# A first weight load split in two and moved from ScalarE's DMA queue to SP's, in a two-layer Mish kernel

## The chip, the cores and the metric

The kernel runs on one core of a Trainium2 chip. The metric is the device time of one execution in microseconds. Before the change it was 105.13 us, the median of three runs (104.34 to 105.44). A core has TensorE (PE), VectorE (DVE), ScalarE (ACT), GpSimd (POOL) and SyncE (SP); each runs its own instructions in order, and they meet at semaphores. SP and ScalarE issue the DMAs here.

## The reference

```python
# x (1, 2048, 512), w1 (512, 1792), b1 (1792,), w2 (1792, 512), all bfloat16
h = jnp.einsum("bsd,df->bsf", x, w1) + b1
sp = jnp.log1p(jnp.exp(-jnp.abs(h))) + jnp.where(h > 0, h, jnp.zeros_like(h))
act = h * jnp.tanh(sp)                       # mish(h)
return jnp.einsum("bsf,fd->bsd", act, w2)
```

## The kernel before

The 2048 tokens are worked in four blocks of 512. In each block the first layer computes, for each of 14 f tiles (128 of the 1792 columns of w1), a 128x512 product over four k tiles (128 of the 512 input features each): `mm1_step`, L194, with w1 as the weights and the transposed x (`xT`) as the moving operand. ScalarE adds b1 and applies Mish (L200) into `a_sb`. The second layer (L252) multiplies `a_sb` with w2 into 128x512 output tiles, which ScalarE (L235) or, at the very end, VectorE (L238) copies out and SP stores (L242). The last ten tokens (eight in the later f tiles) are left out of the first layer's matmuls; VectorE computes them as dot products (`dots`, L213) from a transposed w1 (`w1T`) and broadcast rows of x (`xv`).

TensorE's order around the change: ten warm-up matmuls on constants (L157); eight transposes of the first 256 tokens (L169, `transpose_x`), which need the plain load `x_nat` and an identity from GpSimd; after each group of them VectorE copies the result into `xT` (L173), first k 0, then k 1, then k 2 and 3 together. Then the first layer of block 0 is done for these 256 tokens alone, first for f tiles 0-3 and then for 4-7 (`GROUPS`), and within a group k by k: four matmuls of k 0, four of k 1, and so on, 32 in all, each 256 columns wide. Then come tokens 256-511 for f tiles 0-7 (`xT` loaded by a DMA transpose), then f tiles 8-13 over all 512 tokens.

All loads go through `load` (L92): a DMA start with its own semaphore, which reaches 16 when all has landed. `load_w1` records for each pair (k, f) which semaphore a matmul must wait for. SP issues its loads one after the other from L128 on, ahead of everything else that it does, without waiting for any of them. ScalarE first waits for a memset of `b1_pad` by VectorE (L124), then issues w1's load for k 0-1 of f tiles 0-3, then b1 (L134), then loads its activation table (L151). b1 is turned on VectorE (L263 to L268) before the first Mish needs it.

Of the kernel before, what the change touches and what calls it, by code (L numbers as in the profile page):

```python
# [5 lines left out]
P = 128  # L6
# [28 lines left out]
def bass_standalone__dense_activation_mish__prompt_kernel(  # L35
# [14 lines left out]
    KT, FT = D // P, F // P  # L50
# [7 lines left out]
    with ExitStack() as es:  # L58
        def sb(name, shape, t):
            return es.enter_context(nc.sbuf_tensor(name, shape, t))  # L60
# [5 lines left out]
        b1_nat = sb("b1_nat", [FT, P], BF)  # L66
# [14 lines left out]
        def sem(name):  # L81
            return es.enter_context(nc.semaphore(name))

        sp = Stream(nc.sync, None)
        pe = Stream(nc.tensor, sem("c_pe"))
        dve = Stream(nc.vector, sem("c_dve"))
        act = Stream(nc.scalar, sem("c_act"))
        pool = Stream(nc.gpsimd, sem("c_pool"))

        def load(q, dst, src, name, transpose=False):  # L90
            s = sem(name)
            (q.eng.dma_start_transpose if transpose else q.eng.dma_start)(dst, src).then_inc(s, 16)  # L92
            return (s, 16)
# [3 lines left out]
        def load_w1(q, ks, a, b):  # L97
            t = load(q, w1_sb[:, ks, a * P:b * P], w1v[:, ks, a * P:b * P], "s_w1_%d_%d" % (ks.start, a))
            for f in range(a, b):
                for k in range(ks.start, ks.stop):  # L100
                    t_w1[k, f] = t

        def load_w2(a, b):
            t = load(sp, w2_sb[:, a:b, :], w2v[:, a:b, :], "s_w2_%d" % a)
            for f in range(a, b):
                t_w2[f] = t

        def load_xT(lo, hi):
            t = load(sp, xT[:, :, lo:hi], x2[lo:hi, :], "s_xT%d" % lo, True)
            for j in range(lo // P, hi // P):  # L110
                t_xT[j] = t
# [9 lines left out]
                t_xv[v] = t  # L121

        t_bz = dve.mark(nc.vector.memset(b1_pad[:, :], 0.0))  # L123
        act.wait(t_bz)  # L124

        x01 = x2[0:2 * P, :].rearrange("(p j) d -> p j d", j=2)
        out01 = out2[0:2 * P, :].rearrange("(p j) d -> p j d", j=2)
# [1 line left out]
        for a, b in GROUPS:  # L129
            if a == F0:  # L130
                load_xT(2 * P, 4 * P)
            for ks in (slice(0, 2), slice(2, KT)):
                load_w1(act if (a, ks.start) == (0, 0) else sp, ks, a, b)
        t_b1 = load(act, b1_nat[:, :], b1.rearrange("(j p) -> j p", p=P), "s_b1")  # L134
        load_w2(0, 5)
        load_w2(5, FT)
        load_xv(0, 4)
# [184 lines left out]
```

## Time and profile before

| | |
|---|---|
| median of three runs | 105.13 us (104.34 to 105.44) |
| the profiled execution | 104.65 us, its span 103.4 us |
| TensorE busy | 100.3 us, 97% of the span |
| VectorE, ScalarE busy | 76.9 us, 48.0 us |
| DMA | 11.11 MB moved, 107 GB/s in the mean; 331 to 379 GB/s in most slices of the first seventh |
| chain that ended last | 94% on TensorE, 3% on ScalarE |

Times in a row are microseconds from the span's start unless marked ns. L194 is line 194 of the kernel before. A tile's name in a row leaves numbers out: `w_sb` stands for w1 and w2, `b_nat` for b1. PEld is TensorE's weight load, which runs beside its matmuls. SPq and ACTq rows are the issuing of a DMA on SyncE and ScalarE. A matmul's row shows it longer than the distance to the next one, because they are pipelined: 0.31 us for a step of 0.107. A few matmul records are missing from the trace.

### The profile page before, as it was taken

Reading aid. Unit: us, or ns where it says so; the run is one execution under the profiler, and the core shown is the slowest. Engines: PE = TensorE matmul, PEld = TensorE weight load, DVE = VectorE, ACT = ScalarE, POOL = GpSimd, SP = SyncE. Lnnn points to the kernel's source line nnn. Section 1 sums busy time; section 2 is a strip of 40 time slices with the busy share of each in tenths; the row PEclk is TensorE's granted clock in tenths of the full one; section 3 lists DMA queues with packets and bytes.
Section 4 is the critical chain, followed back from the end, with each engine's and each line's share of the span. In section 5 each row is a group of like instructions: output and inputs, shape, how many; then the busy total and the mean of one; then the engine's idle time right before and its main releaser. Section 6 shows DMA issues by size and latency. Waiting matters only on the chain.

```text
span 103.4 us, 1446 instructions
## 1 busy us (share of the span) xinstructions
PE 100.3 (97%) x518; PEld 50.8 (49%) x526; DVE 76.9 (74%) x254; ACT 48.0 (46%) x75; POOL 0.7 (1%) x6
## 2 busy tenths in 40 slices
PE   6999999999999999999999999999999999999992
PEld 2798744444444444444444444444444444444492
DVE  0340000799999999999999999999999999980011
ACT  1305997201257777222227777522107888720220
POOL 2000000000000000000000000000000000000000
PEclk9999999999999999999999999999999999999999
DMA  2999999999999600011011000001111000001112
GB/s 80 331 294 362 349 379 137 375 262 190 216 245 230 213 6 0 0 51 45 6 51 51 3 0 0 10 0 51 51 51 51 0 0 0 0 6 51 51 51 51
DMA packets 21107, 11.11 MB, mean 107 GB/s; under 512 B 15340, under 2 KB 20716, under 8 KB 21100
## 3 DMA queue, kind: packets, MB, share of 16 engines
q1 hardware_dynamic: 20656, 10.73, 39.0%
q10 hardware_dynamic: 444, 0.29, 1.0%
q8 instruction: 4, 0.07, 0.2%
q14 instruction: 3, 0.02, 0.1%
HBM read 5.25 MB, written 2.10 MB: 71 GB/s over the span
## 4 chain that ended last, share of the span: by engine, by line
PE 94%; ACT 3%; issue 0%; ACTq 0%
PE ps L252 47%; PE ps L194 44%; ACT a_sb L200 3%; PE ps L157 3%; PE ps L169 1%; ACT o_sb L235 0%; ACTq L27 0%
## 5 line engine op out<-in xcount | busy, mean ns | idle before, releaser
L213 DVE SCALAR_TENSOR_TENSOR prod<-w1T,xv 128x512 f32<-128x512 bf16 x120 | 73.6, 684 | 12.2 <-DMA w1T<-in_w_dram 12.2
L194 PE MATMUL ps<-xT,w_sb 128*128 128x512 bf16 (+3 forms) x253 | 49.0, 353 | 0.2
L252 PE MATMUL ps<-w_sb,a_sb 128*128 128x512 bf16 (+3 forms) x247 | 48.6, 355 | 0.3
L200 ACT ACTIVATE a_sb<-ps,b_sb 128x512 bf16<-128x512 f32 (+2 forms) x56 | 37.3, 691 | 13.3 <-PE ps L194 13.3
L194 PEld LDWEIGHTS ps<-xT,w_sb 128*128 128x128 bf16 x256 | 25.1, 99 | 23.2 <-DMA w_sb<-in_w_dram 0.2
L252 PEld LDWEIGHTS ps<-w_sb,a_sb 128*128 128x128 bf16 x252 | 23.6, 98 | 25.2
L235 ACT ACTIVATE o_sb<-ps 128x512 bf16<-128x512 f32 (+1 forms) x16 | 9.2, 575 | 38.2 <-PE ps L252 38.2
L213 DVE DVE_READ_ACCUMULATOR prod<-w1T,xv 128x1 f32 x120 | 9.6, 80 | 0.0
L238 DVE CAST o_sb<-ps 128x256 bf16<-128x256 f32 (+1 forms) x2 | 0.7, 374 | 7.7 <-PE ps L252 7.7
L157 PE MATMUL ps<-const-bfloat16-1.0 128*128 128x512 bf16 (+1 forms) x10 | 2.8, 466 | 0.8 <-PEq L307 0.8
L173 DVE COPY xT<-ps 128x256 bf16<-128x256 bf16 (+1 forms) x3 | 0.9, 336 | 3.1 <-PE ps L169 2.9
L151 ACT ACT_TABLE_LOAD x1 | 1.3, 1283 | 2.2 <-issue 2.2
L157 PEld LDWEIGHTS ps<-const-bfloat16-1.0 128*128 128x128 bf16 x10 | 1.2, 139 | 2.2 <-issue 2.2
L169 PE MATMUL ps<-ident,x_nat 128*128 128x128 bf16 x8 | 1.1, 311 | 0.0
L266 DVE STREAM_TRANSPOSE b_t<-b_pad 32x32 bf16<-32x32 bf16 x4 | 0.8, 202 | 0.1
L169 PEld LDWEIGHTS ps<-ident,x_nat 128*128 128x128 bf16 x8 | 0.9, 147 | 0.0
L123 DVE MEMSET b_pad<- 32x64 uint32 x1 | 0.1, 112 | 0.9 <-PEq L307 0.9
L221 DVE TENSOR_TENSOR hb<-hv,b_sb 128x40 f32<-128x40 f32 (+1 forms) x2 | 0.4, 218 | 0.1
L263 DVE COPY b_pad<-b_nat 14x128 bf16<-14x128 bf16 x1 | 0.2, 182 | 0.3 <-DMA b_nat<-in_b_dram 0.3
L225 ACT ACTIVATE a_sb<-hb 128x40 bf16<-128x40 f32 (+1 forms) x2 | 0.4, 244 | 0.0
L149 POOL TENSOR_SCALAR_AFFINE_SELECT ident<-ones 128x128 bf16<-128x128 bf16 x1 | 0.3, 292 | 0.1
L147 POOL MEMSET ones<- 128x128 bf16 x1 | 0.2, 204 | 0.3 <-POOLq L307 0.3
(5 smaller groups left out, 0.6 us busy)
## 6 DMA issues: line engine op xcount, KB each, us to landing
out_dram<-o_sb SPq DMA_DIRECT2D x15, 128.0 KB, 1.7
w_sb<-in_w_dram SPq DMA_DIRECT2D x1, 1152.0 KB, 10.8
w_sb<-in_w_dram SPq DMA_DIRECT2D x3, 256.0 KB, 4.1
w_sb<-in_w_dram SPq DMA_DIRECT2D x2, 384.0 KB, 4.9
xv<-in_x_dram SPq DMA_DIRECT2D x1, 768.0 KB, 7.6
w_sb<-in_w_dram SPq DMA_DIRECT2D x1, 640.0 KB, 6.6
xv<-in_x_dram SPq DMA_DIRECT2D x1, 512.0 KB, 11.1
x_nat<-in_x_dram SPq DMA_DIRECT2D x1, 256.0 KB, 2.5
```

What stands on the lines that cost most here:

```text
L151: act.eng.preload_act_table(ACT.Mish)
L157: nc.tensor.matmul(ps[:, 7, 0:n], c_w, c_m[:, 0:n], start=True, stop=True)
L169: mm = nc.tensor.transpose(psb[:, (2 * i + j) * P:(2 * i + j + 1) * P], x_nat[:, j, k * P:(k + 1) * P], ident[:, :])
L173: t = dve.mark(nc.vector.tensor_copy(xT[:, ks[0]:ks[0] + n, 0:2 * P], psb[:, 0:2 * n * P].rearrange("p (k t) -> p k t", k=n)))
L194: return nc.tensor.matmul(ps[:, bank, lo:hi], w1_sb[:, k, f * P:(f + 1) * P], xT[:, k, starts[s] + lo:starts[s] + hi], start=first, stop=( ...
L200: t = act.mark(act.eng.activation(a_sb[:, f, starts[s]:starts[s] + width(s, f)], ps[:, bank, 0:width(s, f)], ACT.Mish, bias=b1_sb[:, f:f + ...
L213: t_dot[b] = dve.mark(nc.vector.scalar_tensor_tensor(prod[:, b, :], w1T[:, f, :], 1.0, xv[:, v, :], ALU.mult, ALU.mult, accum_out=hv[:, f, ...
L221: t = dve.mark(nc.vector.tensor_tensor(hb[:, a:b, v:NV], hv[:, a:b, v:NV], b1_sb[:, a:b].unsqueeze(2).to_broadcast([P, b - a, NV - v]), AL ...
L235: t = act.mark(act.eng.activation(o_sb[:, i, lo:hi], ps[:, bank, 0:hi - lo], ACT.Copy))
L238: t = dve.mark(nc.vector.tensor_copy(o_sb[:, i, lo:hi], ps[:, bank, 0:hi - lo]))
L252: mm = nc.tensor.matmul(ps[:, bank, 0:hi - lo], a_sb[:, f, i * P:(i + 1) * P], w2_sb[:, f, lo:hi], start=(f == 0), stop=(f == FT - 1))
L266: t_b1t = dve.mark(nc.vector.transpose(b1_t[c * 32:(c + 1) * 32, :], b1_pad[:, c * 32:(c + 1) * 32]))
```

## The change

The load of w1 for k 0 and 1 of f tiles 0-3 (256 KB) leaves ScalarE. It becomes two loads on SP, k 0 and k 1 apart (128 KB each), directly behind the load of x and ahead of all other loads of w1. ScalarE issues only b1, and without waiting for the memset. A matmul on k 0 now waits for the load of k 0 alone.

```diff
         t_bz = dve.mark(nc.vector.memset(b1_pad[:, :], 0.0))
-        act.wait(t_bz)
+        t_b1 = load(act, b1_nat[:, :], b1.rearrange("(j p) -> j p", p=P), "s_b1")
 ...
         for a, b in GROUPS:
             if a == F0:
                 load_xT(2 * P, 4 * P)
-            for ks in (slice(0, 2), slice(2, KT)):
-                load_w1(act if (a, ks.start) == (0, 0) else sp, ks, a, b)
-        t_b1 = load(act, b1_nat[:, :], b1.rearrange("(j p) -> j p", p=P), "s_b1")
+            for ks in (slice(0, 1), slice(1, 2), slice(2, KT)) if a == 0 else (slice(0, 2), slice(2, KT)):
+                load_w1(sp, ks, a, b)
         load_w2(0, 5)
```

What SP issues from the start of the program, before the change. `128x2x512` is two k tiles of 512 columns, `DMA_TRANSPOSE xT` the tokens 256-511, `x3` three such loads in a row.

```order
L92 DMA x_nat<-in_x_dram 128x1024
L92 DMA w1_sb<-in_w1_dram 128x2x512 x3
L92 DMA_TRANSPOSE xT<-in_x_dram 128x4x256
L92 DMA w1_sb<-in_w1_dram 128x2x768 x2
L92 DMA w2_sb<-in_w2_dram 128x5x512
L92 DMA w2_sb<-in_w2_dram 128x9x512
```

The same place on SP after the change.

```order
L92 DMA x_nat<-in_x_dram 128x1024
L92 DMA w1_sb<-in_w1_dram 128x512 x2
L92 DMA w1_sb<-in_w1_dram 128x2x512 x3
L92 DMA_TRANSPOSE xT<-in_x_dram 128x4x256
L92 DMA w1_sb<-in_w1_dram 128x2x768 x2
L92 DMA w2_sb<-in_w2_dram 128x5x512
L92 DMA w2_sb<-in_w2_dram 128x9x512
```

Two loads of one k tile stand second and third; everything behind them is two places later, in the same order.

TensorE at the first layer's start, before the change, with what each matmul waits for: `s_xn` is x, `s_w1_0_0` the load of w1 that begins at k 0 and f 0, `c_dve` VectorE's copies, `c_pool` the identity.

```order
L169 MATMUL ps<-ident,x_nat 128x128 [waits c_pool,s_xn]
L169 MATMUL ps<-ident,x_nat 128x128 x7
L194 MATMUL ps<-xT,w1_sb 128x256 [waits c_dve,s_w1_0_0]
L194 MATMUL ps<-xT,w1_sb 128x256 x3
L194 MATMUL ps<-xT,w1_sb 128x256 [waits c_dve]
L194 MATMUL ps<-xT,w1_sb 128x256 x3
L194 MATMUL ps<-xT,w1_sb 128x256 [waits c_dve,s_w1_2_0]
```

The same place after the change (two lines are numbered one lower).

```order
L168 MATMUL ps<-ident,x_nat 128x128 [waits c_pool,s_xn]
L168 MATMUL ps<-ident,x_nat 128x128 x7
L193 MATMUL ps<-xT,w1_sb 128x256 [waits c_dve,s_w1_0_0]
L193 MATMUL ps<-xT,w1_sb 128x256 x3
L193 MATMUL ps<-xT,w1_sb 128x256 [waits c_dve,s_w1_1_0]
L193 MATMUL ps<-xT,w1_sb 128x256 x3
L193 MATMUL ps<-xT,w1_sb 128x256 [waits c_dve,s_w1_2_0]
```

No matmul has moved. The four matmuls of k 1 wait for a load of their own, `s_w1_1_0`.

## The prediction

> **What bounds the kernel now.** I read the page first: its first two parts and the shares of the chain.
>
> ```profile
> span 103.4 us, 1446 instructions
> PE 100.3 (97%) x518; PEld 50.8 (49%) x526; DVE 76.9 (74%) x254; ACT 48.0 (46%) x75; POOL 0.7 (1%) x6
> PE 94%; ACT 3%; issue 0%; ACTq 0%
> ```
>
> TensorE is busy 97% of the span and 94% of the chain lies on it, so only something that moves TensorE's stream moves the end. The waits of TensorE and of its weight loads come next (line, what was waited for, total, times, longest).
>
> ```profile
> PE ps L157 <- PEq L307: 0.8, 1, 0.8
> PEld ps L157 <- issue: 2.2, 6, 0.8
> PEld ps L194 <- DMA w_sb<-in_w_dram: 0.2, 1, 0.2
> ```
>
> One wait for data in the whole kernel, and it is the load that the change touches: the first weights of w1 at L194. The chain, in order of time, shows what stands around it (start, length, what).
>
> ```profile
> 0.83 2.83 PE ps L157 x10
> 3.66 0.85 PE ps L169 x8
> 4.51 4.32 PE ps L194 x36
> ```
>
> Ten warm-up matmuls, eight transposes of x, then the first layer, with no gap worth a row. The timeline of TensorE, asked in small windows, sizes the wait and gives the pace on both sides of it. A row covers all matmuls that overlap its window: start of the first, then the time to the end of the last.
>
> ```profile
> 3.45 1.06 PE L169 MATMUL ps<-ident,x_nat 128*128 128x128 bf16 x8
> 4.42 0.13 PEld L194 LDWEIGHTS ps<-xT,w_sb 128*128 128x128 bf16 x2 [0.17 <-DMA w_sb<-in_w_dram]
> 4.42 0.90 PE L194 MATMUL ps<-xT,w_sb 128*128 128x256 bf16 x4
> 4.82 0.61 PE L194 MATMUL ps<-xT,w_sb 128*128 128x256 bf16 x3
> 4.82 3.56 PE L194 MATMUL ps<-xT,w_sb 128*128 128x256 bf16 x30
> L169 PE MATMUL ps<-ident,x_nat x8: 311/311/311, 3.5 to 4.2; 128*128 128x128 bf16 x8
> L194 PE MATMUL ps<-xT,w_sb x30: 272/273/391, 4.8 to 8.1; 128*128 128x256 bf16 x30
> ```
>
> The last transpose starts at 3.45 + 1.06 - 0.31 = 4.20, so they step by 0.75 / 7 = 0.107; the first L194 could start at 4.31 and starts at 4.42. **The wait costs TensorE 0.11 us.** The first and third L194 stand 0.40 apart: 0.20 a step. The fifth, last of the three in the fourth row, starts at 4.82 + 0.61 - 0.27 = 5.16, and the thirtieth of the fifth row at 4.82 + 3.56 - 0.27 = 8.11: 27 steps of 0.109. So TensorE runs at half its pace until shortly before 5.16 (some 4.2 us from its start at 0.83) and the wait lies inside that stretch. The page's clock row is level throughout, so I go by the steps.
>
> **Part 1: the wait goes, if k 0 lands by 4.31.** The issues, from the timeline (start, length), then the landings counted from the issue (in that order x_nat, ScalarE's load, SP's three loads of w1, xT):
>
> ```profile
> 0.80 0.39 SPq L92 DMA_DIRECT2D x_nat<-in_x_dram  x1
> 1.01 0.43 ACTq L92 DMA_DIRECT2D w_sb<-in_w_dram  x1
> 1.25 1.44 SPq L92 DMA_DIRECT2D w_sb<-in_w_dram  x3
> 1.47 0.71 ACTq L92 DMA_DIRECT2D b_nat<-in_b_dram  x1
> 2.73 1.30 SPq L92 DMA_TRANSPOSE xT<-in_x_dram  x1
> 5.73 1.02 SPq L92 DMA_DIRECT2D w_sb<-in_w_dram  x1
> x_nat<-in_x_dram SPq DMA_DIRECT2D x1, 256.0 KB, 2.5
> w_sb<-in_w_dram ACTq DMA_DIRECT2D x1, 256.0 KB, 3.4
> w_sb<-in_w_dram SPq DMA_DIRECT2D x1, 256.0 KB, 3.9
> w_sb<-in_w_dram SPq DMA_DIRECT2D x1, 256.0 KB, 4.1
> w_sb<-in_w_dram SPq DMA_DIRECT2D x1, 256.0 KB, 4.5
> xT<-in_x_dram SPq DMA_TRANSPOSE x1, 5.0
> w_sb<-in_w_dram SPq DMA_DIRECT2D x1, 1152.0 KB, 10.8
> ```
>
> x lands at 3.3, ScalarE's load at 4.4, SP's three at 5.15, 5.8 and 6.7 (issued at 1.25, 1.25 + 0.48 and 1.25 + 2 x 0.48), xT at 7.7. What the DMA engines moved, by stretch:
>
> ```profile
> 0.80:1.80 1.00, 0.97 (x3) 0.43 (x4) 0.11 (x1) 0.00 (x0) 0.49 (x2) 1.00 0.00 0
> 1.80:2.70 0.90, 0.90 (x4) 0.29 (x2) 0.00 (x0) 0.48 (x1) 0.00 (x0) 1.00 0.91 275
> 2.70:3.20 0.50, 0.50 (x4) 0.28 (x3) 0.00 (x0) 0.50 (x1) 0.00 (x0) 1.00 0.74 205
> 3.20:4.30 1.10, 1.10 (x13) 1.04 (x10) 0.39 (x2) 0.30 (x1) 0.00 (x0) 1.00 1.08 377
> 4.30:5.60 1.30, 1.30 (x11) 0.94 (x10) 0.84 (x4) 0.00 (x0) 0.00 (x0) 1.00 0.99 328
> ```
>
> The last figure is GB/s, the one before it the DMA engines' share. Nothing moves for 1.0 us after the first issue; from 3.2 the engines are full. By 2.7 they have moved 248 KB (x is 262 KB), by 3.2 351, by 4.3 766. After the change x and k 0 are 393 KB: passed at 3.2 + 42 / 377 = 3.3. x landed some 0.5 after its last bytes (2.75 to 3.3), so k 0 lands near 3.8 and k 1 (524 KB) near 4.2. Bounds for k 0: as fast as x, 1.25 + 2.5 = 3.75; as slow as SP's first load of w1, 5.15. I take 3.8: that load had 512 KB ahead of it or beside it, k 0 has 256. k 1 is needed four steps later, at 5.1, and is bounded by 4.2 and 1.73 + 4.1 = 5.8. At 5.15 for k 0 the four steps done before 5.16 would be lost: 4 x 0.109 = 0.44. With k 0 at 3.8 L194 starts at 4.31; 0.11 us more at half pace is 0.06 us of later work. **-0.06 us.**
>
> **Part 2: SP issues two loads more**, at 0.48 each, so all that stands behind them on SP's queue starts 0.97 later. The deadlines follow from the steps, less 0.06: k 2-3 of f 0-3 at 5.16 + 4 x 0.109 - 0.06 = 5.54 (its copy of xT, below, ends at 4.97); k 0-1 of f 4-7, twelve steps behind 5.16, at 6.41; k 2-3 of f 4-7, twenty behind, at 7.28; xT for tokens 256-511 at 5.16 + 28 x 0.109 - 0.06 = 8.15. If bytes set the landing, they stay at 5.15, 5.8, 6.7 and 7.7, since as many bytes as before lie ahead of each: all in time by 0.4 to 0.6. If the issue sets it, each comes 0.97 later, at 6.1, 6.8, 7.7 and 8.7: late by 0.56, 0.4, 0.4 and 0.55, and the first lateness covers the others, so at worst +0.6. I take 0: with 1.0 us from issue to first byte, k 0, k 1, k 2-3 and the loads of f 4-7 can start at 2.25, 2.7, 3.2, 3.7 and 4.2, and the bytes ahead of them drain at 2.75, 3.3, 3.7, 4.4 and 5.2. The ring never runs dry; the least cover is 0.4. The Trainium skill (DMA: Bandwidth & Descriptors, Issuing engines are not separate DMA queues) speaks against the change: a second issuing engine buys nothing but sequencer time, and this edit gives just that up. By that rule no byte comes sooner than the ring allows and SP pays 0.97; the 377 GB/s with two queues against 328 with SP's alone bears it out roughly.
>
> Farther back the cover is larger. Rows: w2's second load above (5.73 + 10.8 = 16.5, at worst 17.5), the second layer's start, and the end of VectorE's dots.
>
> ```profile
> 16.89 1.46 PE L252 MATMUL ps<-w_sb,a_sb 128*128 128x512 bf16 x6
> 3.91 1.06 DVE L173 COPY xT<-ps 128x256 bf16<-128x256 bf16 x3 [2.93 <-PE ps L169]
> 6.41 0.17 DVE L268 CAST b_sb<-b_t 128x14 f32<-128x14 bf16 x1
> 8.92 7.13 ACT L200 ACTIVATE a_sb<-ps,b_sb 128x512 bf16<-128x512 f32 x12 [5.42 <-PE ps L194]
> 92.49 0.35 DVE L221 TENSOR_TENSOR hb<-hv,b_sb 128x40 f32<-128x40 f32 x2
> 95.94 0.39 ACT L225 ACTIVATE a_sb<-hb 128x40 bf16<-128x40 f32 x2
> ```
>
> That load of w2 is needed five matmuls after 16.89, at 18.0 (twice the columns of the first steps, twice 0.109 each). The dots end at 92.5 and are used at 95.9: 0.97 is covered.
>
> **Part 3: ScalarE.** Its load of w1 (0.43 us) goes, b1's issue moves from 1.47 to about 0.80, and the wait for VectorE's memset goes. ScalarE's first activation stands at 8.92 after 5.42 idle, and b1 is ready on VectorE at 6.58: 2.3 us of cover, worth nothing. The price is b1's 3.5 KB beside x: 0.01 us at 275 GB/s; if its whole issue of 0.71 came ahead of x, x would land at 4.0 instead of 3.3, against 3.45 when the transposes want it: 0.55 at half pace, +0.28. I take 0: issues of both engines overlapped from 1.25 to 1.44 and SP's were no longer than 0.48.
>
> **Sum**: the profiled execution took 104.65 (103.4 and 1.25 around it): 104.65 - 0.06 = 104.59. The median of the three runs, 105.13, is 0.48 above that execution; from it, 105.07, and I name 105.05.
>
> **The rivals.**
> *No gain (0.12).* k 0 lands no sooner than ScalarE's load did, 4.4, since it is issued 0.24 later (1.25 against 1.01) in one ring. Against it: half the bytes. 105.13.
> *SP's ring runs dry (0.13, slower).* Place: k 2-3 of f 0-3 and xT behind SP's two issues. It decides once a load's start slips by more than the 0.4 us of cover, as it would with issues of 0.71 (b1's row) in place of 0.48. Price 0.6 less 0.06, +0.5: 105.6. For it: the wait is on one queue alone. Against: the full engines from 3.2 on.
> *b1 ahead of x (0.05, slower).* +0.28 - 0.06: 105.35.
> *The pace changes elsewhere (0.10, faster).* Nothing before 4.31 differs on TensorE, so in the profiled execution an earlier change of pace could save at most half of 4.31 to 5.05, 0.37, with the 0.06 in it. In another execution it may come before 4.31 by itself; then TensorE meets the late weights at full pace and the wait is longer: with x at 3.3, transposes at half their step (0.05, two for k 0) and VectorE's copy (1.06 / 3 = 0.35) it could start near 3.8 and waits until 4.4. That is up to 0.6: 104.5. For it: the three runs spread over 1.1 us, which the single wait for data does not explain. The Trainium skill (TensorE: Matmul & The Clock Gate, Part 1: The HAM clock gate) says that the fast clock comes after a free-running window of 3.4 us; by an estimate from that page executions would differ by half a window, 1.7 us, whatever the kernel does, which the runs' 1.1 fits, and no row here shows the window itself.
>
> **How the numbers follow.** The forecast has 0.60 and lies between -0.06 and 0. The rivals reach from 104.5 to 105.6. Three runs spread over 1.1 us leave a median uncertain by some 0.4 by itself, 104.7 to 105.5 around the forecast, so the rivals' ends hold it; I take 104.4 to 105.6. A measurement of this kernel tells some 1%, 1.05 us, from no change. No case reaches that alone; scatter on top of the dry ring or of the pace rival could: 0.07 faster, 0.07 slower, 0.86 within.
>
> **What would show it.** Right: no wait for w_sb on the weight loads; L194 starts at 4.31 (4.3 to 4.35); k 0 landed by 3.9; SP's xT issued near 3.7 and landed by 7.9; TensorE without gaps behind it. Wrong: a wait of L194 for w_sb or xT at 5.1, 5.5 or 8.2 (the dry ring), L169 starting after 3.5 (b1), or w_sb still waited for at 4.3. A shift above 0.6 us with none of these would mean that the pace's change, not the loads, decides.

## The result, and the profile after

The changed kernel takes 105.65 us, the median of 16 runs (105.14 to 106.19); the kernel before, beside it, 104.80 (104.29 to 105.44). The ratio is 1.0083, with a 95% interval of 1.006 to 1.0106: **0.85 us slower**, where 0.06 faster was forecast. Here and below, the median beside a ratio, the ratio and its interval leave out runs more than 1.5% above the fastest of their kernel (one of ten with b1 first, two of four with k 0-3 in one load, four of ten with all loads later), and why those took longer no profile tells. The profiled execution took 105.14 us, its span 103.9.

The shares of the chain on the page of the kernel after:

```profile
PE 89%; DMA 4%; ACT 3%; SPq 1%; issue 1%; ACTq 0%
```

The waits of its TensorE and weight loads for data (total, times, longest):

```profile
PEld ps L193 <- DMA w_sb<-in_w_dram: 1.1, 2, 0.7
PE ps L193 <- DMA w_sb<-in_w_dram: 0.4, 1, 0.4
```

Before, 94% of the chain lay on TensorE and the only wait for data was one of 0.2. Now 4% lie on a DMA and there are two waits. The chain after, in order of time (start, length, what):

```profile
1.72 0.42 SPq L92
2.15 0.04 issue
2.19 3.83 DMA w_sb<-in_w_dram
6.02 0.05 issue
6.07 3.24 PE ps L193 x28
...
77.97 11.89 PE ps L193 x56
```

It no longer begins with TensorE's warm-up but with SP's issues, and crosses to TensorE at 6.07, with the load of k 2-3. Behind that, nothing is different: the last of these rows reads 77.48 and 11.89 before, so 0.49 us were lost early and kept to the end (loads behind them came later too, without a new wait on TensorE). TensorE and its weight loads in that place, from the timeline after:

```profile
4.36 0.60 PE L193 MATMUL ps<-xT,w_sb 128*128 128x256 bf16 x4
5.36 0.61 PE L193 MATMUL ps<-xT,w_sb 128*128 128x256 bf16 x4 [0.41 <-DMA w_sb<-in_w_dram]
4.32 0.34 PEld L193 LDWEIGHTS ps<-xT,w_sb 128*128 128x128 bf16 x4
5.35 0.33 PEld L193 LDWEIGHTS ps<-xT,w_sb 128*128 128x128 bf16 x4 [0.68 <-DMA w_sb<-in_w_dram]
6.06 1.97 PEld L193 LDWEIGHTS ps<-xT,w_sb 128*128 128x128 bf16 x19 [0.38 <-DMA w_sb<-in_w_dram]
```

The four matmuls of k 0 start at 4.36 and do not wait. The four of k 1 start at 5.36, where a step of 0.11 behind the fourth (4.36 + 4 x 0.11 = 4.8) was possible: **0.56 lost**. Those of k 2 start at 6.07 where 5.36 + 4 x 0.11 = 5.8 was: **0.27 lost**. Together 0.83 us. The first four step by (0.60 - 0.27) / 3 = 0.11, so in this execution TensorE was at full pace from 4.36 on, in the profile of before only from about 5.05. That saved half of 0.7, 0.35 us, and had nothing to do with the change, since TensorE's stream is the same up to there. With it the two profiles differ by 0.49; without it they would differ by some 0.84, which is near the 0.85 of the medians. These are one profile of each kernel, so the nearness is no proof.

Where the weights were, from the DMA issues after (in order: k 0, k 1, k 2-3; the last figure is microseconds from issue to landing; issued at 1.26, 1.72 and 2.19):

```profile
w_sb<-in_w_dram SPq DMA_DIRECT2D x1, 128.0 KB, 2.4
w_sb<-in_w_dram SPq DMA_DIRECT2D x1, 128.0 KB, 3.6
w_sb<-in_w_dram SPq DMA_DIRECT2D x1, 256.0 KB, 3.8
```

k 0 lands at 3.7, in time. k 1, as many bytes and issued 0.46 later, lands 1.6 later, at 5.3; k 2-3 at 6.0. What the DMA engines moved meanwhile, by stretch (their share and GB/s are the last two figures):

```profile
1.80:2.70 0.90, 0.90 (x4) 0.29 (x2) 0.00 (x0) 0.90 (x1) 0.00 (x0) 1.00 0.86 246
2.70:3.20 0.50, 0.50 (x5) 0.27 (x3) 0.00 (x0) 0.08 (x1) 0.00 (x0) 1.00 1.00 336
3.20:4.30 1.10, 1.10 (x13) 0.99 (x10) 0.38 (x2) 0.00 (x0) 0.00 (x0) 1.00 0.69 151
4.30:5.60 1.30, 0.90 (x10) 0.54 (x8) 1.08 (x6) 0.00 (x0) 0.00 (x0) 1.00 0.96 331
```

From 3.2 to 4.3 they moved 151 GB/s, where before it was 377. In 1.1 us that is 0.25 MB less, 0.7 us of work at 350 GB/s. Their busy share fell less, from 1.08 to 0.69. So the DMA engines stood idle for a part of the time, and what they moved took 1.6 times as long per byte (0.69 / 151 against 1.08 / 377).

### The profile page after: what moved, and what is told of

Its sections match the earlier page's. It is cut to its first block, busy times and chain, and to the rows that moved or that the text cites. A ratio compares the mean times of both kernels' runs of the same rounds, so it can differ in the third digit from the quotient of the medians.

```text
span 103.9 us, 1448 instructions
## 1 busy us (share of the span) xinstructions
PE 100.2 (97%) x518; PEld 50.4 (49%) x526; DVE 76.8 (74%) x254; ACT 48.1 (46%) x75; POOL 0.7 (1%) x6
## 4 chain that ended last, share of the span: by engine, by line
PE 89%; DMA 4%; ACT 3%; SPq 1%; issue 1%; ACTq 0%
PE ps L251 46%; PE ps L193 43%; DMA w_sb<-in_w_dram 4%; ACT a_sb L199 3%; SPq L92 1%; ACT o_sb L234 0%; ACTq L27 0%
## 5 line engine op out<-in xcount | busy, mean ns | idle before, releaser
L212 DVE SCALAR_TENSOR_TENSOR prod<-w1T,xv 128x512 f32<-128x512 bf16 x120 | 73.6, 689 | 13.3 <-DMA w1T<-in_w_dram 13.3
L212 DVE DVE_READ_ACCUMULATOR prod<-w1T,xv 128x1 f32 x120 | 10.1, 84 | 0.0
```

The costliest lines, as they stand in the source:

```text
L212: t_dot[b] = dve.mark(nc.vector.scalar_tensor_tensor(prod[:, b, :], w1T[:, f, :], 1.0, xv[:, v, :], ALU.mult, ALU.mult, accum_out=hv[:, f, ...
```

## The experiments

The stretch from 3.2 to 4.3 is the measure in all of them, beside the time. Each time is compared with the kernel before on the same chip (104.64 us where no other is given). KB are 1024 bytes here, as in the rows; the expectations count 1000. To starve the DMA engines means here to let them move less than 250 GB/s in that stretch. First theories: **A**, SP's queue alone starves the DMA engines; **B**, two small loads do; **C**, b1 beside x disturbs the first loads.

**b1 first, the rest as before** (one part of the change alone; the later line that loads b1 goes).

```diff
-        act.wait(t_bz)
+        t_b1 = load(act, b1_nat[:, :], ...)      # now ahead of w1's load on ScalarE
```

> The kernel before, with one part of the change: ScalarE issues b1 first and at once, then w1's load for k 0-1 as before. Theory A (one ring: with all of w1 on SP's queue the DMA engines are starved from 3.2 to 4.3, 151 GB/s against 377): w1 is still on two queues, so within 0.2 us of before, the wait for the first w1 load longer by the 0.4 us at most by which its issue moves. Theory B (the split into two loads of 128 KB): same as A. Theory C (b1 issued beside x disturbs the first loads): slower by 0.5 to 0.9 us, and the DMA engines below 250 GB/s between 3.2 and 4.3.

105.12 against 104.64 us, ratio 1.0054 (1.0024 to 1.0084): slower than A and B say, and about as slow as C says. Its DMA stretch:

```profile
3.20:4.30 1.10, 1.10 (x12) 0.86 (x10) 0.24 (x2) 0.02 (x1) 0.00 (x0) 1.00 1.09 381
```

Its loads of k 2-3 on SP and of k 0-1 on ScalarE, with the time from issue to landing:

```profile
w_sb<-in_w_dram SPq DMA_DIRECT2D x1, 256.0 KB, 3.0
w_sb<-in_w_dram ACTq DMA_DIRECT2D x1, 256.0 KB, 3.6
```

The engines are full, so C's disturbance is not there. The loss is mostly another, one wait of 0.7 us for k 0-1 (the only other one, for x, is 0.2), which was issued on ScalarE only at 1.50, behind b1, and landed at 5.1, after SP's k 2-3 (issued 1.26, landed 4.3). The loads came in the order of their issue, across the two queues.

**b1 behind the table load**, otherwise the changed kernel.

```diff
-        t_b1 = load(act, b1_nat[:, :], ...)
+        # the same line, now behind act.eng.preload_act_table(ACT.Mish)
```

> The changed kernel, but ScalarE issues b1 behind its table load, about 2.1 us. Theory A and theory B: as slow as the changed kernel, +0.6 to +1.0 us against before, with waits of 0.3 to 0.6 us for k 1 and k 2-3. Theory C: within 0.2 us of before.

105.61 us, ratio 1.0082 (1.0055 to 1.0109), 117 GB/s. It says nothing on C: the DMA was issued at 0.83 all the same, beside the table load. The test was made again with a wait (GpSimd makes the identity earlier in the program for it):

```diff
+        act.wait(t_id)                            # GpSimd's identity, 1.36 us
         t_b1 = load(act, b1_nat[:, :], ...)
```

> The changed kernel, with b1's issue on ScalarE held back by a wait for GpSimd's identity (in e2_b1_late the DMA was issued at 0.83 us all the same, beside the table load, so that run did not move b1). b1 is issued near 1.4 us, as in the kernel before. Theory A (SP's ring alone starves the DMA engines): +0.6 to +1.0 us against before, below 250 GB/s from 3.2 to 4.3 us. Theory C (b1 beside x is the cause): within 0.3 us of before.

105.91 against 105.05, ratio 1.0096 (1.0074 to 1.0119), with b1 issued at 1.39:

```profile
3.20:4.30 1.10, 1.03 (x13) 0.65 (x10) 0.37 (x2) 0.14 (x1) 0.00 (x0) 1.00 0.64 133
```

The engines starve as in the changed kernel although b1 now comes 0.6 us later, so b1 beside x is not the cause. C falls.

**No split**: k 0 and 1 in one load, second on SP.

```diff
-            for ks in (slice(0, 1), slice(1, 2), slice(2, KT)) if a == 0 else ...:
+            for ks in (slice(0, 2), slice(2, KT)):
                 load_w1(sp, ks, a, b)
```

> The changed kernel with k 0 and k 1 in one load of 256 KB on SP, second behind x. Theory A: +0.6 to +1.0 us against before, the waits for w1 stay. Theory B: within 0.2 us of before, the wait on SP's ring gone with the split. Theory C: +0.5 to +0.9.

105.42 us, ratio 1.0045 (1.0014 to 1.0077). The ratio makes it about half of the loss, the medians (105.42 against 104.64) nearly all of it, so the time leaves open how much of A is right; B's 0.2 is passed by either. One wait for w1 is left, 0.5 us. Its stretch:

```profile
3.20:4.30 1.10, 1.10 (x13) 0.93 (x10) 0.30 (x2) 0.00 (x0) 0.00 (x0) 1.00 0.84 225
```

**The split alone**, both halves on ScalarE.

```diff
-                load_w1(act if (a, ks.start) == (0, 0) else sp, ks, a, b)
+                load_w1(act if a == 0 and ks.start < 2 else sp, ks, a, b)   # ks: 0, 1, 2-3
```

> The kernel before with its load for k 0-1 split in two, both on ScalarE, b1 third as before. Theory A: within 0.2 us of before, perhaps 0.06 faster. Theory B: +0.5 to +1.0 us. Theory C: within 0.2 us.

104.90 us, ratio 1.0031 (1.0002 to 1.006):

```profile
3.20:4.30 1.10, 1.10 (x12) 0.91 (x10) 0.28 (x2) 0.69 (x1) 0.00 (x0) 1.00 1.08 374
```

The engines are full: splitting alone does not starve them, and B falls. The one wait for w1 in its profile, 0.4 us, is order again: k 1, issued at 1.42 behind SP's k 2-3 (1.26), landed 3.7 later, near 5.2.

So far A stands, but its size varies with what is in the first loads. That gave two finer forms. **A1**: the third load on a queue comes late, and a second queue hides it. **D**: a load issued after 1.5 to 1.7 us comes late on either queue, and what matters is how many bytes were issued until then.

**k 1 alone back on ScalarE**, behind b1.

```diff
-                load_w1(sp, ks, a, b)
+                load_w1(act if (a, ks.start) == (0, 1) else sp, ks, a, b)
```

> The changed kernel with k 1 alone moved back to ScalarE, second there behind b1, issued near 1.5 us; k 2-3 becomes the third load on SP, near 1.72. Theory A1 (the third load on a ring brings its first bytes only near 4.2 us; a second ring hides it): k 1 moves from 3.3 on and lands by 4.3, no wait for it; k 2-3 lands at 5.3 to 6.0 and costs 0 to 0.5 us; +0.0 to +0.5 against before. Theory D (any load issued after 1.5 to 1.7 us takes over 2 us to its first bytes, on either ring): k 1 lands at 5 or later, a wait of 0.3 us or more for it, +0.6 to +1.0.

104.95 against 105.05 us, ratio 1.0006 (0.9981 to 1.003): the loss is gone. k 1 landed at 4.3, as A1 says; D's "at 5 or later" missed, with k 1 issued at 1.49. Only k 2-3 was still waited for, 0.3 us. **The same, k 1 issued later**: ScalarE waits for the identity first.

```diff
+        act.wait(t_id)
         t_b1 = load(act, b1_nat[:, :], ...)       # k 1 behind it, at 2.06 instead of 1.49
```

> As g1_k1_act, but ScalarE first waits for GpSimd's identity, so that k 1 is issued near 2.1 us, later than the changed kernel issues it on SP (1.72). Theory A1: k 1 still moves from 3.3 on and lands by 4.5, no wait of more than 0.1 us for it; +0.0 to +0.5 us. Theory D: first bytes over 2 us behind the issue, so it lands at 4.9 or later and costs 0.4 us or more; +0.6 to +1.2.

108.69 against 105.05 us, ratio 1.0381 (1.0327 to 1.0435), much worse than either theory's figure. k 1's issue and its landing in the first of the two kernels:

```profile
1.49 0.37 ACTq L92 DMA_DIRECT2D w_sb<-in_w_dram  x1
```

```profile
w_sb<-in_w_dram ACTq DMA_DIRECT2D x1, 128.0 KB, 2.8
```

The same two rows of the second:

```profile
2.06 0.42 ACTq L92 DMA_DIRECT2D w_sb<-in_w_dram  x1
```

```profile
w_sb<-in_w_dram ACTq DMA_DIRECT2D x1, 128.0 KB, 5.5
```

Its DMA stretch, and TensorE where it waits for k 1:

```profile
3.20:4.30 1.10, 1.10 (x12) 0.83 (x10) 0.20 (x1) 0.59 (x1) 0.00 (x0) 1.00 0.80 205
```

```profile
7.65 4.02 PE L194 MATMUL ps<-xT,w_sb 128*128 128x256 bf16 x20 [2.52 <-DMA w_sb<-in_w_dram]
```

Issued 0.57 later on the same queue, with the same load ahead of it there, the 128 KB land 3.3 later, at 7.6. Part of that is order: SP's k 2-3, issued at 1.72, now stood ahead of k 1 and landed at 5.8. A1 falls all the same, since it had k 1 land by 4.5: a second queue does not save a late load. D's wording fails as well. The trace has k 1's first packets at 3.6, 1.6 us after the issue and not over 2; fourteen of the sixteen counts of its semaphore came by 6.1, the last two at 7.3 and 7.6. The last row shows the rest of the price: after 2.5 us without work TensorE is back at half pace, 20 matmuls with (4.02 - 0.27) / 19 = 0.20 a step. The page of this run has the granted clock at 5 tenths in the slice from 8.1 to 10.7 us and at 9 in all others.

**One queue, but more bytes early**: k 0-3 in one load of 512 KB, second on SP.

```diff
-            for ks in (slice(0, 1), slice(1, 2), slice(2, KT)) if a == 0 else ...:
+            for ks in (slice(0, KT),) if a == 0 else (slice(0, 2), slice(2, KT)):
                 load_w1(sp, ks, a, b)
```

> The changed kernel with all of k 0-3 of f 0-3 in one load of 512 KB, second on SP. Theory A1 and theory D: the second load has enough bytes to cover the third, so the DMA engines move over 330 GB/s from 3.2 to 4.3 us; k 0-3 lands near 5.1, TensorE waits once, for 0.6 to 0.8 us; loads behind it land no later than before; +0.3 to +0.6 us against before. Theory F (one ring is slow whatever stands in it): below 250 GB/s from 3.2 to 4.3 us, k 0-3 lands at 5.8 or later, +0.9 us or more.

Its DMA stretch, and the landing of that load (issued at 1.26):

```profile
3.20:4.30 1.10, 1.10 (x12) 0.87 (x10) 0.24 (x2) 0.00 (x0) 0.00 (x0) 1.00 1.00 339
```

```profile
w_sb<-in_w_dram SPq DMA_DIRECT2D x1, 512.0 KB, 4.2
```

With all of w1 on SP, the engines stay busy and the 512 KB land at 5.5, later than the 5.1 of A1 and D and sooner than F's 5.8. So a single queue is not enough to starve them. TensorE waits 1.1 us once, for all of them together, longer than the 0.6 to 0.8 expected. The four runs took 105.09, 105.40, 107.2 and 107.51 us against 105.05, too few and too scattered for an interval.

**k 2-3 on ScalarE at once**, k 0 and k 1 on SP.

```diff
-                load_w1(sp, ks, a, b)
+                load_w1(act if (a, ks.start) == (0, 2) else sp, ks, a, b)   # b1 behind it
```

> The changed kernel with k 2-3 of f 0-3 on ScalarE, first there and at once (0.80), b1 second; k 0 and k 1 stay second and third on SP. Loads issued before 1.7 us hold 655 KB (x, k 2-3, k 0), between the 524 of g1_k1_act (328 GB/s from 3.2 to 4.3) and the 786 of before (377). Theory D: 330 to 380 GB/s from 3.2 to 4.3, the engines thin out only behind 4.0; loads land in the order of issue, so k 0 lands near 4.4 and k 1 between 4.8 and 5.8; 0.0 to +0.6 us against before, less than the changed kernel's +0.85.

104.89 against 104.73 us, ratio 1.0024 (0.9996 to 1.0051). k 0, issued at 1.26 behind k 2-3, landed at 4.85, later than the expected 4.4, and k 1 at 5.3. The time, and the rate below, are as D says. The DMA stretch:

```profile
3.20:4.30 1.10, 0.96 (x10) 0.70 (x8) 0.07 (x1) 0.12 (x1) 0.00 (x0) 1.00 1.10 366
```

**All loads 0.6 us later**, to see from when "late" counts.

```diff
-        act.wait(t_bz)
+        act.wait(t_id); sp.wait(t_id)             # first loads at 1.39
```

> The kernel before with all loads held back by 0.6 us: SP and ScalarE wait for GpSimd's identity before their first load (x and k 0-1 near 1.4, k 2-3 near 1.85, the next near 2.3). Theory D1 (late is counted from the first bytes: loads issued within about 1 us of the first issue come in one stream, later ones wait): all stretches shift by 0.6, the DMA engines move over 330 GB/s from 3.8 to 4.9; k 0-1 lands near 5.0, +0.4 to +0.8 us. Theory D2 (late is counted from the program's start: what is issued after 1.7 comes late): k 2-3, issued at 1.85, brings its first bytes over 2 us later, below 270 GB/s from 3.8 to 4.9, +1.0 us or more.

105.3 against 104.73 us, ratio 1.0048 (1.0019 to 1.0077); its ten runs reach from 104.79 to 107.52. Its stretch, 0.6 later as well:

```profile
3.80:4.90 1.10, 0.83 (x8) 0.77 (x8) 0.40 (x2) 0.11 (x1) 0.00 (x0) 1.00 1.09 378
```

k 2-3, issued at 1.85 here, landed 3.9 later, as in the profile of before, and the engines stayed full; the time is as D1 says. So what counts is not a time in the program but the time behind the first load (D1).

**The wait alone taken away**: ScalarE's load of k 0-1 as before, without waiting for the memset.

```diff
-        act.wait(t_bz)
```

> The kernel before with one part of the change that is worth keeping by theory D: ScalarE no longer waits for the memset, so its load of k 0-1 is issued near 0.80 instead of 1.01; nothing else moves. Theory D: 786 KB are still issued by 1.7 us, the DMA engines stay full from 3.2 to 4.3 (over 340 GB/s), k 0-1 lands some 0.1 to 0.2 us sooner; 0.0 to 0.2 us faster than before. If the wait hid something: slower by 0.1 us or more.

104.93 against 104.73 us, ratio 1.0022 (0.9998 to 1.0046), 383 GB/s. The load lands no sooner than in the second profile of before, below (4.3 against 4.2), and there is no gain; whether it costs something the interval does not tell.

**The kernel before, once more**, for a second profile.

> The kernel before once more, for a second profile of it. All theories: 104.3 to 105.5 us; from 3.2 to 4.3 over 340 GB/s; a wait for the first w1 load between 0.1 and 0.5 us, no other wait on TensorE.

104.91 us. TensorE at the place of the wait:

```profile
3.49 1.04 PE L169 MATMUL ps<-ident,x_nat 128*128 128x128 bf16 x8
4.36 1.02 PE L194 MATMUL ps<-xT,w_sb 128*128 128x256 bf16 x4
```

In this execution there is no wait for w1 at all, against the 0.1 to 0.5 us expected: the first L194 starts 0.15 behind the last transpose, as in the changed kernel.

Put together, with the bytes of the loads that were issued up to 1.5 us:

```
                              queues   KB issued by 1.5   GB/s, 3.2 to 4.3
b1 behind the table load        1          384                 117
b1 behind a wait                1          384                 133
changed kernel                  1          384                 151
k 1 on ScalarE at 2.06          2          384                 205
no split                        1          512                 225
k 1 on ScalarE at 1.49          2          512                 328
k 2-3 on ScalarE at once        2          640                 366
k 0-3 in one load               1          768                 339
split alone                     2          768                 374
before, again                   2          768                 371
before                          2          768                 377
b1 first                        2          768                 381
wait taken away                 2          768                 383
```

The kernel with all loads 0.6 us later fits with 768 KB and 378 GB/s in its shifted stretch. Neither the number of queues nor the size of a load alone orders these rows; the bytes issued early come nearest to it. x alone is 256 KB of them. At equal bytes, though, the rows with two queues are the higher ones each time: 205 against 117 to 151, 328 against 225, 371 to 383 against 339. They differ in the number or the size of their loads as well, so what a second queue adds by itself was not separated.

The packets in the traces show more than the rate. Of the 1 KB packets, which are w1's, that began between 3.2 and 4.3 us, the median took 46 ns in every run of the table. In each of the five rows up to 225 GB/s seven to nine packets took over 0.25 us, nine in the changed kernel; there were four in the row with 328, one each in those with 339 and 366, and none in the five with 371 to 383. k 1 of the changed kernel did not begin late: its packets move from about 3.2 on, right behind k 0's. Its semaphore made five of the sixteen counts by 4.2 and the other eleven from 4.6 to 5.3, so a part of the load was held up. Which load suffers varies: with b1 behind the table load k 1 landed at 5.8 and k 2-3 at 6.6, with b1 behind a wait at 4.9 and 6.8.

## Why the prediction was wrong

**What bounds the kernel** was right: TensorE's stream, and the early wait as the only place where a load reaches it.

**Part 1, k 0**: right. Forecast to land near 3.8, it landed at 3.7 and the wait was gone. Its worth was misjudged all the same: the 0.11 us came from one execution, and a second profile of the same kernel has no such wait. There was next to nothing to win. L194 could not start at 4.31 either: without any wait it started at 4.36, in the profile after and in the second one of before, 0.15 behind the last transpose, where one step of 0.11 was taken.

**Part 1, k 1, and Part 2: here the prediction failed**, in the sentence "with 1.0 us from issue to first byte, k 0, k 1, k 2-3 and the loads of f 4-7 can start at 2.25, 2.7, 3.2, 3.7 and 4.2 ... The ring never runs dry". It let every load start 1.0 us behind its issue, or when the bytes ahead had drained, and then move at the full rate of before. The starts held for k 0 and k 1 (k 1's packets move from 3.2 on, its turn was forecast for 3.3). The rate did not: the DMA engines, taken as full from 3.2 on because they are so before, moved 151 GB/s in place of 377. k 1, forecast for 4.2, landed at 5.3; k 2-3, forecast for 5.15, at 6.0. Before the change three loads of 256 KB are issued by 1.25 us; the change left two, of 256 and 128 KB, which by the table goes with a slow stretch. The upper bounds of the text, 5.8 for k 1 and 6.1 for k 2-3, held. For k 1 it had even named a bound of 5.8 beside a need at 5.1, and no case put a price on that. (The least cover in that sentence's own figures is 0.5, not 0.4; nothing hangs on it.)

**The rival "SP's ring runs dry"** is what happened, with a chance of 0.13. Its price, +0.5, was too low: it counted the lateness of k 2-3 and left out k 1, and in the profile k 1 cost 0.56 and k 2-3 another 0.27. That the measured 105.65 lies so near to its 105.6 is luck: that figure stood on the 105.13 of three runs, where sixteen gave 104.80. Its condition was wrong too: it asked for issues of 0.71 in place of 0.48, and SP's took 0.41 to 0.47. Its naming of one queue was at best half of it: one queue with 768 KB early moved 339 GB/s, and two with 384 KB moved 205.

**The rule of the Trainium skill** on issuing engines (DMA: Bandwidth & Descriptors, Issuing engines are not separate DMA queues) was cited as speaking against the change, and then priced at nothing. It says that a second issuing engine saves only the sequencer's time, which is usually small beside the DMA itself. The runs agree in so far as the bytes issued in the first 0.7 us come nearest to ordering the rows; that two queues moved more at equal bytes they leave unexplained, and the 377 GB/s with two queues against 328 with one, which the prediction read as roughly bearing the rule out, point that way too. The loss here, 0.85 us, was not small beside the 0.06 that was sought.

**Part 2, xT and farther back**: xT, forecast to stay at 7.7, landed at 3.69 + 4.7 = 8.4 and was not waited for, since TensorE was late itself. Farther back the cover held: the transposed w1 came 1.1 later (VectorE waits 13.3 us for it, before 12.2) and the last operation of the dots began at 93.2 in place of 92.5, with their use at 96.4. **Part 3**: right, b1's move costs and brings nothing (b1 behind a wait loses as much as the changed kernel). **The pace**: it changes where it will, before 4.36 in the profile after, near 5.05 in that of before, but 16 runs of each kernel hold that scatter, and the interval lies clear of 1.

What stays open is why a load that is issued later than about 0.9 us behind the first comes so late when little is under way: with 768 KB early, loads were issued as late, and the DMA engines still moved 328 to 357 GB/s from 4.3 to 5.6. It was seen on both queues and for 128 and 256 KB. Why single packets then take up to 0.9 us, and whether they cause the low rate or go along with it, no run tells.

## What to carry to other kernels

At the start of a program, count the bytes that all queues together have issued within the first 0.7 us of loading; in this kernel 768 KB kept the DMA engines full from 3.2 to 4.3 us and 384 KB did not. A second queue is worth having there, since it gets more issued in that time. Order the first loads by need across all queues, since they landed in the order of issue in every run here. And take a wait of 0.1 us from one profile as a gain only after a second profile shows it too.

## What the hardware showed that was not expected

- The time from issue to landing of 128 KB of w1 grew with the issue time in the kernels that had up to 512 KB under way: 2.4 to 2.7 us issued at 1.26, 2.8 at 1.49, 3.2 to 4.1 at 1.72, 5.5 at 2.06.
- Where less than 250 GB/s were moved, seven to nine packets of 1 KB took 0.25 to 0.91 us in that stretch, against a median of 46 ns; at 371 to 383 GB/s none did.
- Loads landed in the order of issue across the two queues: with b1 first, one issued 0.24 us earlier on the other queue landed whole before the later one (4.3 against 5.1).
- A DMA written behind the table load on ScalarE was issued at 0.83 us, before that load had ended.
- After a wait of 2.5 us TensorE was back at half pace, steps of 0.20 instead of 0.11.
